# Loading x ahead of the DMA transposes, tile 3 by PE, padded K rows and a second store queue in an attention plus GLU kernel

## The chip, the cores and the metric

The kernel runs on one core of one Trainium2 chip. The metric is the device time of one execution in microseconds (us). "Span" is the time from the first to the last instruction in a profile of such an execution; it is mostly 1.7 to 2.1 us shorter than the device time of the same execution. Every execution also carries a mean granted TensorE clock, where 1.000 is full speed. Engines: PE is TensorE (matmul), DVE is VectorE, ACT is ScalarE, POOL is GpSimd, SP is SyncE, which only issues DMAs here.

## The reference

Layer norm of x, sliding dilated attention (32 heads of 20, a window of 8 keys at distance 2), and a gated bilinear unit on the un-normalized layout, summed with x. S = 2048, D = 640, F = 1536, all bf16.

```python
xn = layernorm(x)                       # x: (1, 2048, 640)
q, k, v = split(xn @ wqkv)              # 32 heads of 20
logits = q . k[s - 2*w], w = 0..7       # masked where s - 2*w < 0
A = (softmax(logits * 20**-0.5) . v[s - 2*w]) @ wo
B = ((xn @ w_gate) * (xn @ w_up)) @ w_down
return x + A + B
```

## The kernel before

The sequence is cut into 16 tiles of 128 rows. For each tile DVE takes mean and variance of a row (`ln_stats_a/b`, `ln_aggr`), normalizes (`ln_apply`), and the result XNS must be transposed into XNT, because PE needs the model dimension on partitions. Tiles 0, 1 and 2 are transposed by PE (through PSUM, copied out by ACT and DVE), tiles 3 to 15 by a DMA transpose that SP issues. The x loads, the weight loads and the transposes stand in one program order on SP's queue; some x loads are issued by ACT. PE projects Q and K of tiles 0 to 5 tile by tile, of tiles 6 and 7 with matmuls 256 wide, and of tiles 8 to 15 with matmuls 512 wide, which need four tiles at once.

```python
    x_load(1, "act"); x_load(0)
    # ... wqkv for Q, x 2 and 3, wqkv for K ...
    for t in range(4, 8):
        x_load(t)

    def ln_apply(t, between=None):
        # ... XNS[t % 4] = (x - mean) * rstd, on DVE ...
        if t >= NTP:                                    # NTP = 3
            o = XNT[:, :, t * TS:(t + 1) * TS]
            op("sp", lambda e: e.dma_start_transpose(o, xs), r=[xs], w=[o], dma=True, name=f"xT{t}")
        for u in {3: (8, 9), 4: (10,), 5: (11, 12), 6: (13,), 7: (14,), 8: (15,)}.get(t, ()):
            x_load(u, "act" if u > 11 else "sp")        # tiles 12 to 15 from ACT

    # order of the projections: (which, tile in the pair); which 0 is Q, 1 is K
    order = ((0, 0), (0, 1), (1, 0), (1, 1)) if t0 < 2 else ((0, 0), (1, 0), (0, 1), (1, 1))
    # ... tail(): the last row tile is stored in three pieces, all from SP
```

XNS has four buffers, so the normalization of tile t + 4 waits until the transpose of tile t has read its buffer. A small scheduling layer records all operations and turns overlaps of 64-byte pieces of memory into semaphore waits.

Of the kernel before, what the change touches and what calls it, by code (L numbers as in the profile page):

```python
# [18 lines left out]
PAD = (W - 1) * DIL  # L19
NT = 16  # L20
NJ = 4
TS = 128
JB = 512
DHALF = D // 2
# [4 lines left out]
HS = S // 2  # L29
SB = 256  # L30
NSB = HS // SB
KL = PAD + HS

ENGINES = ("sp", "act", "pe", "dve", "pool")
ROW_BYTES = {}
# [177 lines left out]
def build_kernel(nc, A_x, A_wqkv, A_wo, B_x, B_w_gate, B_w_up, B_w_down, out):  # L213
# [32 lines left out]
    for h in range(2):  # L246
# [3 lines left out]
        QH.append(sb(f"QH{h}", [128, NCH, HS]))  # L250
        KH.append(sb(f"KH{h}", [128, NCH, KL]))
    a_ht = place[0]
# [12 lines left out]
    NXS = 14  # L265
    XST = sb("XST", [128, NXS, D], at=a_log)
    NXN = 4
    NTP = 3
    XNS = sb("XNS", [128, NXN, D], at=a_log + NXS * D * 2)
    NXR = 2  # L270
    TLAST = 12
# [17 lines left out]
    xhbm = A_x[0]  # L289
    ohbm = out[0]  # L290

    def dma(o, i, r=(), w=(), name="", eng="sp", group=None):
        return op(eng, lambda e: e.dma_start(o, i), r=r, w=w, dma=True, name=name, group=group)
# [7 lines left out]
       r=[IDENT[:]], w=[IDENT[:]], name="ident")  # L301
# [7 lines left out]
    def x_load(t, eng="sp"):  # L309
        dma(XST[:, t % NXS, :], xhbm[t * TS:(t + 1) * TS, :], w=[XST[:, t % NXS, :]], name=f"xld{t}", eng=eng)  # L310

    wqkv_src = A_wqkv.rearrange("(c p) n -> p c n", p=128)

    def wqkv_load(g, c=None, eng="sp"):
# [12 lines left out]
        wqkv_load(1, c)  # L327
    for t in range(4, 8):
        x_load(t)

    later = []

# [24 lines left out]
    def ln_stats_a(t):  # L357
        if t >= NT:
            return
        x, st = XST[:, t % NXS, :], STATS[:, t % 2, 0:12]  # L360
        op("dve", lambda e: e.bn_stats(st[:, 0:6], x[:, 0:DHALF]), r=[x], w=[st], name=f"bna{t}")  # L361

    def ln_stats_b(t):
        if t >= NT:
            return
        x, st = XST[:, t % NXS, :], STATS[:, t % 2, 0:12]
        op("dve", lambda e: e.bn_stats(st[:, 6:12], x[:, DHALF:D]), r=[x], w=[("stb", t)], name=f"bnb{t}")  # L367

    def ln_aggr(t):
        if t >= NT:  # L370
            return
        st, mv, sd = STATS[:, t % 2, 0:12], MV[:, t, 0:2], SD[:, t, 0:1]
        op("dve", lambda e: e.bn_aggr(mv, st), r=[st, ("stb", t)], w=[mv], name=f"bnag{t}")  # L373
        op("act", lambda e: e.activation(sd, mv[:, 1:2], ACT.Sqrt, bias=EPSC[:, 0:1]), r=[mv, EPSC[:]], w=[("sd", t)],  # L374
           name=f"sd{t}")
# [13 lines left out]
    def ln_rstd(t):  # L389
        if t >= NT:  # L390
            return
        sd, rstd = SD[:, t, 0:1], SD[:, t, 1:2]
        op("dve", lambda e: e.reciprocal(rstd, sd), r=[("sd", t)], w=[("rstd", t)], name=f"rstd{t}")  # L393

    def ln_apply(t, between=None):
        if t >= NT:
            return
        x, xs, mv = XST[:, t % NXS, :], XNS[:, t % NXN, :], MV[:, t, 0:2]
        sd, rstd = SD[:, t, 0:1], SD[:, t, 1:2]
        op0 = ALU.add if t == 1 else ALU.subtract  # L400
        mean = ("nm", t) if t == 1 else mv
        if between is None:
            ln_rstd(t)
        else:
            between()
        for c0, c1 in ((0, 128), (128, D)) if t == 0 else ((0, D),):
            o, i = xs[:, c0:c1], x[:, c0:c1]
            op("dve", (lambda o, i: lambda e: e.tensor_scalar(o, i, mv[:, 0:1], rstd, op0=op0, op1=ALU.mult))(o, i),  # L408
               r=[i, mean, ("rstd", t)], w=[o], name=f"lnap{t}")
        if t >= NTP:  # L410
            o = XNT[:, :, t * TS:(t + 1) * TS]
            op("sp", lambda e: e.dma_start_transpose(o, xs), r=[xs], w=[o], dma=True, name=f"xT{t}")
        for u in {3: (8, 9), 4: (10,), 5: (11, 12), 6: (13,), 7: (14,), 8: (15,)}.get(t, ()):
            x_load(u, "act" if u > 11 else "sp")
        if t == NT - 1:
            late_loads()

# [230 lines left out]
    stores = []  # L648
    fin_bank = [0]

    def tail(t, nb):
        j, rows = t // 4, slice((t % 4) * TS, (t % 4 + 1) * TS)
        flush_h(0)
        n = NF + NCH
        last = t == NT - 1
        parts = ((0, DHALF - 64), (DHALF - 64, 64)) if last and nb == 1 else ((0, DHALF),)
        for h, wid in parts:
            b = bank()
            c0 = nb * DHALF + h
            cols = slice(c0, c0 + wid)  # L660
            for i in range(n):
                if i < NF:
                    l, x = ht(j, i)[:, rows], WD[:, i, cols]
                else:
                    l, x = VO[:, i - NF, t * TS:(t + 1) * TS], WO[:, i - NF, cols]
                op("pe", (lambda l, x, i, b, wid: lambda e: e.matmul(PS[:, b, 0:wid], l, x, start=(i == 0), stop=(i == n - 1)))(l, x, i, b, wid),  # L666
                   r=[l, x], w=[PS[:, b, :]], name=f"dn{t}_{nb}_{i}")
            if t < TLAST:
                if nb == 0:
                    fin_bank[0] = b  # L670
                    continue
                assert b == fin_bank[0] + 1
                o = FACC[:, t % NFO, :].rearrange("p (n d) -> p n d", n=2)
                i = PS[:, b - 1:b + 1, 0:wid]
                op("act", (lambda o, i: lambda e: e.activation(o, i, ACT.Copy))(o, i),  # L675
                   r=[PS[:, b - 1, :], PS[:, b, :]], w=[o], name=f"fin{t}")
                continue
            o = FOUT[:, t % NFO, cols]
            xr = XR[:, t % NXR, cols]
            op("dve", (lambda o, xr, b, wid: lambda e: e.tensor_tensor(o, PS[:, b, 0:wid], xr, ALU.add))(o, xr, b, wid),  # L680
               r=[PS[:, b, :], xr], w=[o], name=f"fin{t}_{nb}")
            if last:
                stores.append(dma(ohbm[t * TS:(t + 1) * TS, cols], o, r=[o], name=f"odma{t}_{c0}"))
        if nb == 1 and t < TLAST:
            if t % 2 == 0:
                return
            f = FACC[:, (t - 1) % NFO:(t - 1) % NFO + 2, :]
            d = ohbm[(t - 1) * TS:(t + 1) * TS, :].rearrange("(u p) n -> p u n", p=TS)
            stores.append(op("pool", lambda e: e.dma_start(d, f, accum_op=ALU.add), r=[f, ("out",)], w=[("out", t)],  # L689
                             dma=True, name=f"oacc{t}"))  # L690
        elif nb == 1 and not last:
            f = FOUT[:, t % NFO, :]
            stores.append(dma(ohbm[t * TS:(t + 1) * TS, :], f, r=[f], name=f"odma{t}"))
            if t + NXR < NT:
                xr_load(t + NXR)
# [20 lines left out]

    def tr(t):
        ln_pe(t)
        if t == 1:
            ln_copy(t)  # L720
        if t < 3:
            ln_stats_a(t + 1)
            ln_stats_b(t + 1)
            ln_aggr(t + 1)
        if t > 1:
            ln_copy(t)
        if t < 3:
            ln_apply(t + 1)

    n_ln = [4]  # L730
    t_ln = [12.3]

    def ln_pace(t):
        while t_ln[0] <= t and n_ln[0] < NT:
            u = n_ln[0]
            if u == 4:
                ln_stats_a(4)
                ln_stats_b(4)
                ln_aggr(4)
            ln_stats_a(u + 1)  # L740
            ln_stats_b(u + 1)
            ln_rstd(u)
            ln_apply(u, lambda: ln_aggr(u + 1))
            n_ln[0] += 1
            t_ln[0] += 1.45

    tp = 6.8
    for t0 in (0, 2, 4):
        bm = bank() if t0 == 4 else None
        if t0 == 2:  # L750
            bank_ring[:] = [5, 0, 6, 7, 2, 1, 3, 4]
            bm = bank()
        order = ((0, 0), (0, 1), (1, 0), (1, 1)) if t0 < 2 else ((0, 0), (1, 0), (0, 1), (1, 1))
        at = {(0, 0): (3, lambda: tr(1)), (1, 0): (3, lambda: tr(2))}
        for which, dt in order:
            t = t0 + dt
            b = bank()
            if t0 == 0:
                if bm is None:
                    bm = bank()  # L760
                proj_tile(which, t, b, bm, (2 * which + t) * TS, at.get((which, t)))
            else:
                proj_part(which, t, (0, 1), b, 0)
                proj_part(which, t, (2, 3), b, 2 * TS)
                proj_part(which, t, (4,), bm, (2 * which + dt) * TS)
            part_evac(which, t, 1, 0, 4, b, 0)
            tp += 1.4
            if (which, dt) == (1, 1):
                for u in (0, 1):
                    part_evac(u, t0, 2, 4, 1, bm, 2 * u * TS)  # L770
            ln_pace(tp)
# [19 lines left out]
    def exp_preload():  # L791
        op("act", lambda e: e.activation(DUM[:, 0:1], EPSC[:, 0:1], ACT.Exp), r=[EPSC[:]], w=[DUM[:]], name="exp_preload")

    t_pe, t_dve = [31.0], [33.2]
    fill, pos = [], [0]
    pv_done = [0]
    loaded = []
# [164 lines left out]
```

## Time and profile before

| | before |
|---|---|
| device time, median of the first 3 runs | 256.66 us (256.22 to 256.66) |
| span of the profiled run | 254.3 us, clock 1.000 |
| PE busy | 98% |
| first real matmul of the projections / last matmul | 6.1 us / 251.9 us |

The page of the profile, busy time of the engines and the chain of work that ended last by engine (shares of the span):

```profile
PE 249.0 (98%) x1618; PEld 148.8 (59%) x1618; DVE 215.4 (85%) x251; ACT 114.2 (45%) x203; POOL 35.9 (14%) x44
...
PE 92%; DMA 5%; DVE 1%; ACT 1%; issue 0%; SPq 0%
```

PE is the limit. The 5% of DMA in the chain is, in order of time, the first x load (2.72 us), the load of tile 10 (4.28) and the transpose of tile 7 behind it (5.50); the last two are what the change aims at. The view of waits of PE shows where PE stands still for a transpose (us in total, times, longest):

```profile
PE PS L478 <- DMA XNT<-XNS: 1.6, 1, 1.6
PE PS L441 <- DVE EPSC L297: 1.0, 1, 1.0
```

L478 is the tile-by-tile projection, `XNT<-XNS` a DMA transpose. The timeline of PE shows where it is (start us, us, engine, line, operation, what, count, idle time before):

```profile
12.29 8.54 PE L478 MATMUL PS<-XNT,WQKV 128*128 128x128 bf16 x150
22.48 2.96 PE L478 MATMUL PS<-XNT,WQKV 128*128 128x128 bf16 x50 [1.65 <-DMA XNT<-XNS]
25.57 5.66 PE L496 MATMUL PS<-XNT,WQKV 128*128 128x256 bf16 x50
31.06 1.24 PE L463 MATMUL PS<-XNT,WQKV 128*128 128x512 bf16 x5
```

The matmuls of tile 5 start at 22.48 although the ones before were through at 20.83. The transposes of tiles 4 to 7, issued between 14.4 and 20.1 us, and how long they took from issue to landing:

```profile
L412 SPq DMA_TRANSPOSE XNT<-XNS x4: 1205/1250/1742, 14.5 to 20.0; - x4
...
DMA to landing us min/median/max: 2.9/5.7/6.9
```

One by one, from the semaphore increments in the trace (a DMA counts its semaphore up in 16 steps; at the sixteenth it has landed): tile 4 took 2.91 us, tile 5 5.98, tile 6 6.90, tile 7 5.50. The DMA queues between 17 and 19 us (q1 is SP's queue, q10 ACT's, q8 fetches instructions; packets, MB, share of the 16 engines' time in this stretch, over 100% where packets overlap):

```profile
q1 hardware_dynamic: 513, 0.26, 90.7%
q10 hardware_dynamic: 148, 0.17, 61.5%
q8 instruction: 1, 0.02, 2.8%
```

The end of the kernel: the last two stores are issued one behind the other by SP, the second one at 252.30 (in the trace), 0.1 us after its data.

```profile
251.92 0.81 SPq L293 DMA_DIRECT2D out_dram<-FOUT  x2
251.97 0.23 DVE L680 TENSOR_TENSOR FOUT<-PS,XR 128x64 bf16<-128x64 f32 x1
```

### The profile page before, as it was taken

Reading aid. Unit: us, or ns where it says so; the run is one execution under the profiler, and the core shown is the slowest. Engines: PE = TensorE matmul, PEld = TensorE weight load, DVE = VectorE, ACT = ScalarE, POOL = GpSimd, SP = SyncE. Lnnn points to the kernel's source line nnn. Section 1 sums busy time; section 2 is a strip of 40 time slices with the busy share of each in tenths; the row PEclk is TensorE's granted clock in tenths of the full one; section 3 lists DMA queues with packets and bytes.
Section 4 is the critical chain, followed back from the end, with each engine's and each line's share of the span. In section 5 each row is a group of like instructions: output and inputs, shape, how many; then the busy total and the mean of one; then the engine's idle time right before and its main releaser. Section 6 shows DMA issues by size and latency. Waiting matters only on the chain.

```text
span 254.3 us, 3924 instructions
## 1 busy us (share of the span) xinstructions
PE 249.0 (98%) x1618; PEld 148.8 (59%) x1618; DVE 215.4 (85%) x251; ACT 114.2 (45%) x203; POOL 35.9 (14%) x44
## 2 busy tenths in 40 slices
PE   8997999999999999999999999999999999999996
PEld 3996955555554444444444447764444777777775
DVE  4795999999999962999999995799999999996221
ACT  6574666555555557555555552325555112112000
POOL 1000001024344422002222101101000010111000
PEclk9999999999999999999999999999999999999999
DMA  6799869947784673264458961294000021430511
GB/s 204 262 179 186 106 125 400 313 126 134 144 146 80 128 124 62 76 256 83 82 106 253 403 227 24 18 359 59 0 0 0 3 19 33 54 39 15 103 52 53
DMA packets 26369, 32.01 MB, mean 126 GB/s; under 512 B 10576, under 2 KB 22864, under 8 KB 26320
## 3 DMA queue, kind: packets, MB, share of 16 engines
q1 hardware_dynamic: 19392, 21.64, 28.0%
q0 software_dynamic: 6240, 9.31, 23.4%
q10 hardware_dynamic: 720, 0.82, 1.6%
q8 instruction: 12, 0.20, 0.3%
q14 instruction: 5, 0.04, 0.0%
HBM read 14.42 MB, written 4.59 MB: 75 GB/s over the span
## 4 chain that ended last, share of the span: by engine, by line
PE 92%; DMA 5%; DVE 1%; ACT 1%; issue 0%; SPq 0%
PE PS L635 41%; PE PS L666 29%; PE PS L463 17%; DMA XST<-in_A_x_dram 3%; PE PS L489 2%; PE PS L496 2%; DMA XNT<-XNS 2%; DVE XNS L408 0%; PE PS L422 0%; ACT KH L504 0%; ACT XNS L381 0%; DVE SD L393 0%; DVE STATS L361 0%; DVE STATS L367 0%; ACT SD L374 0%; DVE MV L373 0%
## 5 line engine op out<-in xcount | busy, mean ns | idle before, releaser
L635 PE MATMUL PS<-XNT,WU 128*128 128x512 bf16 x240 | 59.6, 379 | 0.0
L635 PE MATMUL PS<-XNT,WG 128*128 128x512 bf16 x240 | 59.6, 379 | 0.0
L602 DVE TENSOR_TENSOR PVB<-VO,ATB 128x10240 f16<-128x10240 bf16 x8 | 43.9, 5489 | 0.2
L463 PE MATMUL PS<-XNT,WQKV 128*128 128x512 bf16 x200 | 43.3, 379 | 0.0
L666 PE MATMUL PS<-WD,HT 128*128 128x320 bf16 (+2 forms) x300 | 43.2, 294 | 0.0
L635 PEld LDWEIGHTS PS<-XNT,WU 128*128 128x128 bf16 x240 | 23.5, 98 | 28.3
L635 PEld LDWEIGHTS PS<-XNT,WG 128*128 128x128 bf16 x240 | 23.5, 98 | 28.2
L637 ACT ACTIVATE USX<-PS 128x512 bf16<-128x512 f32 x48 | 28.7, 597 | 22.6 <-PE PS L635 22.1
L666 PEld LDWEIGHTS PS<-WD,HT 128*128 128x128 bf16 x300 | 28.7, 98 | 11.0
L463 PEld LDWEIGHTS PS<-XNT,WQKV 128*128 128x128 bf16 x200 | 23.5, 118 | 19.5
L597 DVE TENSOR_TENSOR PVB<-PVB 128x5120 f16<-128x5120 f16 (+1 forms) x16 | 34.5, 2156 | 0.3
L530 POOL DMA_DIRECT2D LOG<-PE x24 | 21.6, 928 | 60.3 <-DMA LOG<-PE 60.1
L637 ACT ACTIVATE HT<-PS 128x512 bf16<-128x512 f32 x36 | 21.5, 597 | 16.3 <-PE PS L635 16.3
L675 ACT ACTIVATE FACC<-PS 128x640 f16<-128x640 f32 x12 | 8.5, 704 | 44.3 <-PE PS L666 44.3
L666 PE MATMUL PS<-WO,VO 128*128 128x320 bf16 (+2 forms) x165 | 27.1, 295 | 0.0
L666 PEld LDWEIGHTS PS<-WO,VO 128*128 128x128 bf16 x165 | 15.9, 98 | 5.9
L519 DVE TENSOR_TENSOR TMP<-QH,KH 128x2048 f16<-128x2048 bf16 x16 | 19.1, 1219 | 0.0
L519 DVE TENSOR_TENSOR PP<-QH,KH 128x2048 f16<-128x2048 bf16 x16 | 18.9, 1219 | 0.0
L524 DVE TENSOR_TENSOR PP<-PP,TMP 128x4096 f16<-128x4096 f16 x8 | 18.3, 2291 | 0.2
L530 POOL DMA_DIRECT2D PE<-PP x8 | 8.7, 1090 | 63.6 <-DVE PP L525 63.6
L689 POOL DMA_DIRECT2D out_dram<-FACC x6 | 7.1, 1186 | 74.7 <-ACT FACC L675 74.7
L680 DVE TENSOR_TENSOR FOUT<-PS,XR 128x320 bf16<-128x320 f32 (+2 forms) x9 | 4.1, 455 | 15.3 <-PE PS L666 15.2
(67 smaller groups left out, 227.0 us busy)
## 6 DMA issues: line engine op xcount, KB each, us to landing
PE<-PP POOLq DMA_DIRECT2D x8, 512.0 KB, 5.0
ATB<-LOG SPq DMA_DIRECT2D x8, 512.0 KB, 4.3
LOG<-PE POOLq DMA_DIRECT2D x24, 128.0 KB, 2.7
WG<-in_B_w_gate_dram SPq DMA_DIRECT2D x5, 384.0 KB, 6.3
WU<-in_B_w_up_dram SPq DMA_DIRECT2D x5, 384.0 KB, 11.1
WD<-in_B_w_down_dram SPq DMA_DIRECT2D x1, 1920.0 KB, 10.3
out_dram<-in_A_x_dram SPq DMA_DIRECT2D x1, 1920.0 KB, 9.2
out_dram<-FACC POOLq DMA_DIRECT2D x6, 320.0 KB, 4.9
```

The costliest lines, as they stand in the source:

```text
L463: op("pe", (lambda l, x, c: lambda e: e.matmul(PS[:, b, :], l, x, start=(c == 0), stop=(c == NCH - 1)))(l, x, c), r=[l, x], w=[PS[:, b, :] ...
L489: op("pe", (lambda o, l, x, st, sp: lambda e: e.matmul(o, l, x, start=st, stop=sp))(o, l, x, st, sp), r=[l, x], w=[o], name=f"pp{which}_{m ...
L519: return (1.22, lambda: op("dve", lambda e: e.tensor_tensor(o, qw, kw, ALU.mult), r=[q, k], w=[o], name=f"prod{h}_{p}_{c}"))
L524: (2.3, lambda: op("dve", lambda e: e.tensor_tensor(a, a, b, ALU.add), r=[a, b], w=[a], name=f"psum{h}_{p}")),
L530: op("pool", lambda e: e.dma_start(o, i, accum_op=ALU.add), r=[o, i], w=[o], dma=True, name=name)
L597: return lambda: op("dve", lambda e: e.tensor_tensor(o, x, y, ALU.add), r=[x, y], w=[o], name=f"{name}_{b}")
L602: lambda: op("dve", lambda e: e.tensor_tensor(PVB[:], vw, aw, ALU.mult), r=[v, a], w=[PVB[:]], name=f"pv_{b}")),
L635: op("pe", (lambda l, x, c: lambda e: e.matmul(PS[:, b, :], l, x, start=(c == 0), stop=(c == NCH - 1)))(l, x, c), r=[l, x], w=[PS[:, b, :] ...
L637: op("act", lambda e: e.activation(o, PS[:, b, :], ACT.Copy), r=[PS[:, b, :]], w=[o], name=f"guev{which}_{m}_{j}")
L666: op("pe", (lambda l, x, i, b, wid: lambda e: e.matmul(PS[:, b, 0:wid], l, x, start=(i == 0), stop=(i == n - 1)))(l, x, i, b, wid), r=[l, ...
L675: op("act", (lambda o, i: lambda e: e.activation(o, i, ACT.Copy))(o, i), r=[PS[:, b - 1, :], PS[:, b, :]], w=[o], name=f"fin{t}")
L689: stores.append(op("pool", lambda e: e.dma_start(d, f, accum_op=ALU.add), r=[f, ("out",)], w=[("out", t)], dma=True, name=f"oacc{t}"))
```

## The change

The intent is to have x in SBUF before the transposes start, so that no load stands between transposes 4 to 7, with tiles 8 to 11 and 14, 15 loaded in pairs. Tile 3 is transposed by PE, so that SP's queue has no transpose in it until tile 4. All x loads but that of tile 1 are now issued by SP: ACT no longer issues loads 12 to 15. KH rows are padded to a multiple of 64 bytes. The next to last store piece goes out from ACT. Constants of the static scheduler are adjusted.

```diff
-KL = PAD + HS
+KL = (PAD + HS + 31) // 32 * 32
-    NTP = 3
+    NTP = 4
+    def x_load2(t):
+        dst = XST[:, t % NXS:t % NXS + 2, :]
+        dma(dst, xhbm[t * TS:(t + 2) * TS, :].rearrange("(u p) n -> p u n", p=TS), w=[dst], name=f"xld{t}")
     for t in range(4, 8):
         x_load(t)
+    x_load2(8)
+    x_load2(10)
+    x_load(12)
@@ ln_apply
-        for u in {3: (8, 9), 4: (10,), 5: (11, 12), 6: (13,), 7: (14,), 8: (15,)}.get(t, ()):
-            x_load(u, "act" if u > 11 else "sp")
+        if t == 7:
+            x_load(13)
+            x_load2(14)
@@ tail
-                stores.append(dma(ohbm[...], o, r=[o], name=f"odma{t}_{c0}"))
+                eng = "act" if c0 == DHALF else "sp"
+                stores.append(dma(ohbm[...], o, r=[o], name=f"odma{t}_{c0}", eng=eng))
@@ order of the projections; tile 3 is transposed inside the last one of tiles 0 and 1
-        order = ((0, 0), (0, 1), (1, 0), (1, 1)) if t0 < 2 else ((0, 0), (1, 0), (0, 1), (1, 1))
-        at = {(0, 0): (3, lambda: tr(1)), (1, 0): (3, lambda: tr(2))}
+        order = ((0, 0), (0, 1), (1, 0), (1, 1)) if t0 < 4 else ((0, 0), (1, 0), (0, 1), (1, 1))
+        at = {(0, 0): (3, lambda: tr(1)), (1, 0): (3, lambda: tr(2)), (1, 1): (4, lambda: tr(3))}
-    t_pe, t_dve = [31.0], [33.2]
+    t_pe, t_dve = [30.3], [31.2]
# cut: tr() and ln_pace() in the form that fits tile 3 on PE, t_ln 12.3 -> 12.6
```

More of the change, by code (lines that the diff above doesn't have):

```diff
@@ L682, in tail @@
             if last:
-                stores.append(dma(ohbm[t * TS:(t + 1) * TS, cols], o, r=[o], name=f"odma{t}_{c0}"))
+                eng = "act" if c0 == DHALF else "sp"
+                stores.append(dma(ohbm[t * TS:(t + 1) * TS, cols], o, r=[o], name=f"odma{t}_{c0}", eng=eng))
         if nb == 1 and t < TLAST:
@@ L718, in tr @@
         ln_pe(t)
-        if t == 1:
+        if t != 2:
             ln_copy(t)
-        if t < 3:
-            ln_stats_a(t + 1)
-            ln_stats_b(t + 1)
-            ln_aggr(t + 1)
-        if t > 1:
+        ln_stats_a(t + 1)
+        ln_stats_b(t + 1)
+        ln_aggr(t + 1)
+        if t == 2:
             ln_copy(t)
@@ L730, in build_kernel @@
     n_ln = [4]
-    t_ln = [12.3]
+    t_ln = [12.6]
     def ln_pace(t):
@@ L735, in ln_pace @@
             u = n_ln[0]
-            if u == 4:
-                ln_stats_a(4)
-                ln_stats_b(4)
-                ln_aggr(4)
             ln_stats_a(u + 1)
```

## The prediction

> **What bounds the kernel now.** TensorE does: the page shows PE busy 98% of a 254.3 us span, and the chain that ended last is 92% PE. The view of PE's waits has two entries: 1.0 us at the start (before any data exists) and one stall of 1.6 us, "PS L478 <- DMA XNT<-XNS". The timeline puts it at 20.83 to 22.48 us: the projection of tile 5 waits for its DMA transpose. From 25.57 us (after a second wait of some 0.13 us for tiles 6 and 7) to 251.9 us PE never stops. So only the head (0 to 31 us) and the last store can pay.
>
> **Cause of the stall.** Read issue by issue, the DMA records show that transposes issued while no x load is in flight, or before it, land 2.7 to 2.9 us after issue (tile 3, tile 4). Those of tiles 5, 6 and 7, issued at 16.4, 18.2 and 20.0 us between the x loads of tiles 10 to 15, take 6.0, 6.9 and 5.5 us, and the loads take 4.5 to 5.4 instead of 2.7 to 4.0. VectorE, not PE alone, then waits: 1.0 us twice before the normalization of tiles 9 and 10, for their buffers, which those late transposes are still reading. The Trainium skill (DMA: Bandwidth & Descriptors, Rules for kernel authors) says a transpose next to ordinary DMAs "needs nothing"; that is about correct data, and this trace shows that it costs time.
>
> **What the change does, with costs.**
> - Loads of tiles 8 to 12 go out before any transpose. x loads stream at about 0.45 us a tile (landings of tiles 4 to 7: 10.86 to 12.17), so they should be in by about 14.5 us. Transposes 4 to 7 then run without loads: about 2.8 us each. Tile 4 issued near 14.0 lands near 17 (wanted 18.3); tile 5 near 18.3 (wanted 21.1); tile 7 near 21 (wanted 24.0). The 1.65 + 0.13 us stall goes.
> - Tile 3 by PE: five more 128x128 transposes, 0.28 us of PE (as for tiles 1 and 2 in the chain), plus one 0.69 us eviction on ACT, which has slack.
> - Loads 13 and 14+15 are still before transposes 8 to 11; those are wanted at about 29.4 us instead of 31.06. I expect tile 11 in by 27 to 29: little margin, the main risk.
> - VectorE's normalizations end about 2 us earlier, so the logits start near 30.4 instead of 32.13. PE's program after the head is unchanged.
> - KH padding: the products take 1.22 us before, and rows 64-byte aligned should not change that; it removes false dependencies only. About 0.
> - Last store: the 16 KB store was issued at 252.30, 0.1 us after its data, behind the other store's issue. Two queues: 0.1 to 0.15 us. The skill (same page, "Issuing engines are not separate DMA queues") says two issuers save only issue time, which is this size.
>
> **Sum on the critical path.** -1.78 + 0.28 - 0.12 = -1.6 us of 256.66: 255.1 us, with 254.3 to 256.1 in 8 of 10. Faster by over 2%: 1%; within 2%: 98%; slower: 1%.
>
> **What would show it.** No PE wait for XNT in the head; transposes of tiles 4 to 7 under 3.5 us; the 256-wide projections start at 24.0 (before 25.57) and the 512-wide ones at 29.4 (before 31.06); the span falls by the same amount; last store issued by 252.2 minus that shift.
>
> **What would make it wrong.** Transposes 8 to 11 slowed by loads 13 to 15, so PE stalls before the 512-wide projections (gain 0.8 us or less); transposes slow of themselves, not through mixing; a new wait in mid-kernel from the shifted VectorE order.

## The result and the profile after

The kernel after takes 254.49 us (median of 6 runs, 254.27 to 254.76), against 256.66 us (6 runs, 256.22 to 257.52). Ratio 0.9911, 95% interval 0.9895 to 0.9927: 0.9% less, inside the range. Ratios here are the mean time of one kernel's fast runs over that of the other's of the same rounds, so not quite the ratio of the medians.

The page after (the lines that answer to those of before):

```profile
PE 249.1 (99%) x1623; PEld 149.3 (59%) x1623; DVE 214.7 (85%) x251; ACT 114.8 (45%) x204; POOL 35.9 (14%) x44
...
PE 99%; DVE 0%; issue 0%
```

The chain is PE alone now, with 5 more matmuls (the transposes of tile 3). Of PE's waits only the one at the start is left:

```profile
PE PS L449 <- DVE EPSC L297: 1.0, 1, 1.0
```

The timeline of PE over the same stretch:

```profile
12.68 11.33 PE L486 MATMUL PS<-XNT,WQKV 128*128 128x128 bf16 x200
23.85 5.62 PE L504 MATMUL PS<-XNT,WQKV 128*128 128x256 bf16 x50
29.31 2.97 PE L471 MATMUL PS<-XNT,WQKV 128*128 128x512 bf16 x13
```

The 200 narrow matmuls run without a break, the 512-wide ones start 1.75 us earlier (31.06 to 29.31), and nothing waits after that: the last matmul of the chain ends at 250.19 instead of 251.95. Transposes 4 to 7:

```profile
L419 SPq DMA_TRANSPOSE XNT<-XNS x4: 1198/1266/1452, 14.2 to 18.6; - x4
...
DMA to landing us min/median/max: 2.9/3.3/4.3
```

One by one: 2.95, 4.33, 3.56 and 2.86 us. The queues between 17 and 19 us have no q10 any more, but the instruction fetch is still there:

```profile
q1 hardware_dynamic: 1065, 0.27, 100.2%
q8 instruction: 1, 0.02, 3.3%
```

The end:

```profile
250.17 0.35 ACTq L293 DMA_DIRECT2D out_dram<-FOUT  x1
250.46 0.33 SPq L293 DMA_DIRECT2D out_dram<-FOUT  x1
```

So the span fell by 1.8 us (254.3 to 252.5), about what was predicted (1.6), while the median times fell by 2.2. Two questions are left: what exactly made the transposes slow, since tile 5's still takes 4.33 us although the last load landed at 16.58, 0.7 us after its issue; and where the other 0.4 us come from. (The profiled execution of before took 256.07 us, 0.6 us less than the median from which the prediction subtracts; that of after, 254.55, lies at its median.)

### The profile page after: what moved, and what is told of

Same layout as the page of the kernel before. It is cut to its first block, busy times and chain, and to the rows that moved or that the text cites. A ratio compares the mean times of both kernels' runs of the same rounds, so it can differ in the third digit from the quotient of the medians.

```text
span 252.5 us, 3929 instructions
## 1 busy us (share of the span) xinstructions
PE 249.1 (99%) x1623; PEld 149.3 (59%) x1623; DVE 214.7 (85%) x251; ACT 114.8 (45%) x204; POOL 35.9 (14%) x44
## 4 chain that ended last, share of the span: by engine, by line
PE 99%; DVE 0%; issue 0%
PE PS L643 41%; PE PS L674 29%; PE PS L471 17%; PE PS L486 4%; PE PS L497 2%; PE PS L504 2%; PE PS L449 2%; PE PS L430 1%; DVE FOUT L688 0%; DVE ZERO L296 0%; DVE EPSC L297 0%
```

## The experiments

Theories at the outset. A: any x load among the transposes slows them; the change takes the loads out. F (B in the first runs): DMA fetches of instructions slow them, loads do not matter. C: moving tile 3 to PE is what helped. D: the padding or the store queue carries a part. A further one, R, came later. "Wanted" in the expectations is the time at which PE would come to the tile if nothing had stalled it. "One run" means a single profiled execution: its latencies and stalls can be read, its time carries no interval.

**Loads alone.** Kernel before with the new loads, tile 3 still by DMA.

```diff
+    x_load2(8)
+    x_load2(10)
+    x_load(12)
-        for u in {3: (8, 9), 4: (10,), 5: (11, 12), 6: (13,), 7: (14,), 8: (15,)}.get(t, ()):
-            x_load(u, "act" if u > 11 else "sp")
+        if t == 7:
+            x_load(13)
+            x_load2(14)
```

> Kernel before with the x loads of the change alone (8 to 12 ahead, 13 and 14+15 behind transpose 7); tile 3 is still transposed by DMA. Theory A (x loads among the transposes cost the stall; the PE transpose of tile 3 is only what makes room for it): transposes 5 to 7 take 3 to 4.4 us instead of 5.5 to 6.9, the stall before tile 5 goes, but tile 3's transpose now stands behind loads that land until 16.6 us in the kernel after, so it lands at 16 to 17 us instead of 14.4 and PE, which wants it at 15.14, stalls 1 to 2 us there: time within 0.4 us of before. Rival B (the loads do not matter, the DMA instruction fetches do): tile 3's transpose takes 2.7 us as before and there is no stall at tile 3, or the stall before tile 5 stays.

Measured: 255.41 us (4 runs: 255.40, 255.41, 255.41 and 258.04), ratio 0.9978, interval 0.9909 to 1.0047. In the profile tile 3's transpose took 5.91 us behind the loads, which landed until 16.87, and PE waited 1.9 us for it; transposes 4 to 6 took 3.2, 2.6 and 2.6 us, and 7, with a fetch at 19.91 in its flight, 4.0. As expected: the loads ahead of the transposes free tiles 5 to 7 and bury tile 3 (the median time, 0.7 us under before, fell more than the 0.4 that was expected at most). The PE transpose of tile 3 is what makes room.

This profile (the 258.04 us run) shows a second effect. Its granted clock is 0.993, and by stretches (columns: us, busy PE, PEld, DVE, ACT, POOL, then granted clock, DMA share, GB/s):

```profile
15.00:18.40 3.40, 1.48 (x27) 1.33 (x25) 3.40 (x14) 1.29 (x4) 0.00 (x0) 1.00 0.61 116
18.40:21.80 3.40, 3.40 (x36) 3.40 (x34) 1.24 (x4) 0.61 (x2) 0.00 (x0) 0.50 0.95 92
21.80:25.00 3.20, 3.20 (x60) 3.20 (x59) 1.85 (x8) 2.43 (x7) 0.00 (x0) 1.00 0.61 166
```

From 0.9 us after the stall PE ran 3.4 us at half clock: 36 matmuls in 3.4 us, against 60 in the 3.2 us after it. Half of 3.4 us is a loss of 1.7 us, on top of the stall.

**Tile 3 by PE alone.** Kernel after with the loads put back among the transposes (12 to 15 from ACT), no padding, one store queue.

```diff
-    x_load2(8)
-    x_load2(10)
-    x_load(12)
-        if t == 7:
-            x_load(13)
-            x_load2(14)
+        for u in {3: (8, 9), 4: (10,), 5: (11, 12), 6: (13,), 7: (14,), 8: (15,)}.get(t, ()):
+            x_load(u, "act" if u > 11 else "sp")
-KL = (PAD + HS + 31) // 32 * 32
+KL = PAD + HS
-                eng = "act" if c0 == DHALF else "sp"
+                eng = "sp"
-    t_pe, t_dve = [30.3], [31.2]
+    t_pe, t_dve = [31.0], [33.2]
```

> Kernel before with tile 3 transposed by PE alone: x loads 8 to 15 stand among the transposes as before, no KH padding, one store queue. Theory A: transposes 5 to 7 still take 5 us or more, PE stalls 1 to 1.5 us before tile 5 or 6, and 0.28 us of PE transposes come on top: time 0 to 0.4 us above before. Rival C (taking tile 3 out of the DMA transposes is what freed the queue): the stall goes and the time falls by 1.2 us or more.

Measured: 255.77 us (255.04 to 256.60), ratio 0.9978, interval 0.9915 to 1.0041; span of the profiled run 253.2. Neither side was right. Transposes 5, 6 and 7 are still slow (5.42, 4.91, 4.02 us), but the stall before tile 5 shrank; the chain (start us, us, what) shows 0.8 us of it (0.5 by the view of waits, which showed 1.65 before):

```profile
12.85 8.11 PE PS L482 x145
20.96 0.02 issue
20.98 0.60 ACT KH L508
21.58 0.19 ACT SD L378
21.77 2.94 PE PS L482 x50
```

The profile puts this wait down to ACT; tile 5's transpose landed at 21.62 in the trace, so I take it to be the transpose. With tile 3 off SP's queue, loads 8 and 9 were issued at 8.8 instead of 13.1 us. My expectation of no gain or a loss was a miss in the profile; in the times the interval leaves it open.

**One batch behind tile 3.** Kernel after, tile 3 by DMA as before, loads 8 to 15 as four pairs right behind it.

```diff
-    NTP = 4
+    NTP = 3
-    x_load2(8)
-    x_load2(10)
-    x_load(12)
-        if t == 7:
-            x_load(13)
-            x_load2(14)
+        if t == 3:
+            for u in (8, 10, 12, 14):
+                x_load2(u)
# and tr(), order and at of the kernel before
```

> Kernel after, but tile 3 by DMA transpose as before (no PE transposes of it), and all x loads 8 to 15 as four pairs in one batch right behind that transpose and ahead of transpose 4. Theory A: tile 3 lands by 14.5 as in before, the batch lands between about 15 and 18.5, transposes 4 and 5 suffer a little from it (4 to 5 us), tile 4 lands at 18.5 to 19 against 18.0 wanted: stall 0.5 to 1 us, later ones none; time 255.3 to 255.9, no better than after. If the loads cost nothing to transposes of their own queue that stand behind them: no stall, 0.28 us under after (span near 252.2).

Measured: 260.18 us (259.82 to 260.77), ratio 1.0141, interval 1.0087 to 1.0195: slower by 1.4%, much more than expected. The batch landed only at 21.54, with an instruction fetch at 19.49 in it; transpose 4 behind it took 6.85 us; PE stalled 4.2 us, and the clock fell (0.987 to 0.993 in all four runs). Here the transpose behind the loads on its own queue landed only after all of them. Why the last two pairs took 1.8 and 2.4 us each, where the second took 0.9, I did not settle.

**All loads ahead.** Kernel after, loads 13 to 15 also ahead of transpose 4.

```diff
-        if t == 7:
+        if t == 3:
             x_load(13)
             x_load2(14)
```

> Kernel after with loads 13 and 14+15 also ahead of transpose 4. Theory A: with no load in flight, transposes 8 to 11 take 2.7 to 2.9 us except one that an instruction fetch (16 KB packet) falls into (4 us or more); in the kernel after they took 3.2 to 4.6. PE does not wait for them in either: span within 0.1 us of 252.5. If the loads land later than 17 us, transpose 4 is late (over 3.5 us) and PE may stall at tile 4 (wanted 18.3). Rival B: the latencies of transposes 8 to 11 do not change.

Measured: one run, 254.78 us, span 252.7, no stall. The transposes issued from 20 to 26 us (8 to 11) took 2.6, 2.8, 3.8 and 3.3 us (kernel after: 3.8, 4.6, 3.8, 3.2). The slow one, tile 10's, is the one with a fetch (24.72 us) in its flight. Both the loads and the fetch are visible; PE waits for neither. Tile 5's transpose, issued at 16.14 with loads landing until 17.04, still took 4.40 us, with a fetch at 18.14.

**Moving the fetches.** In both kernels the warm-up gets more PE instructions for the same time, so that PE's 16 KB instruction fetches come at other moments.

```diff
-    warm(10)
+    warm_waits(30, 2)      # 30 matmuls 128 wide, each behind two waits that are already satisfied
+    warm(2)
```

> Kernel before with more PE instructions in the warm-up (30 narrow matmuls with 2 satisfied waits each and 2 wide ones for 10 wide ones): the same work follows, but PE's instruction fetches (16 KB packets, at 10.95, 17.99, 26.74 us before) come 1 to 5 us earlier. The x loads stand as before. Theory F (the fetch at 18 us freezes the transpose of tile 5; loads among transposes add little): with the fetch out of 16.4 to 20.5 us, tile 5's transpose lands 3 to 4.4 us after issue, no stall before tile 5, time 1.0 us or more under before. Theory A (loads among transposes): it still takes 5 us or more and PE stalls 1 us or more before tile 5 or 6. Both in part: 4.4 to 5 us, stall 0.2 to 0.8. If PE starts its real work later than 5.6 us, the wanted times shift by that.

> Kernel after with the same longer warm-up. No x load is in flight from 16.6 to 20 us. Theory F: the transpose that took 4.33 us (tile 5, fetch at 17.92) takes 2.6 to 3.2 us now, and the 1 to 1.5 us go to whichever transpose the moved fetch falls into (probably tile 4 or tile 7). If transposes slow down for another reason: tile 5 still takes over 4 us. Span 252.3 to 253.2: a fetch in tile 4's transpose can make PE wait some tenths at tile 4 (wanted 18.3).

Measured for the kernel after: one run, 254.15 us, span 252.4. The fetch moved from 17.92 to 15.09 us; PE's first projection started at 6.0, as before. The transposes of tiles 4 to 7:

```profile
L419 SPq DMA_TRANSPOSE XNT<-XNS x4: 1276/1299/1467, 14.2 to 18.6; - x4
...
DMA to landing us min/median/max: 2.6/2.8/3.6
```

Tile 5's took 2.86 us instead of 4.33, tile 4's, into which the fetch now fell, 3.60 instead of 2.95. No load moved in the program, but the loads of tiles 8 to 12 landed by 15.27 instead of 16.58, since the fetch before this one moved too. The run without padding and second store queue (below) excludes that this is what helped: there the loads were in by 15.29, no load was in flight, the fetch came at 18.12, and tile 5's transpose took 4.10 us. So the fetch is a cause.

The trace hints at how. In the kernel after, an ordinary load under a fetch (tiles 8 and 9, fetch at 12.79) had 15 of its 16 semaphore increments by 13.57 us and the last at 15.24. Tile 5's transpose under the fetch at 17.92 had all 16 increments between 20.11 and 20.23, and 19 of its 256-byte packets on SP's queue, starting at 18.85 to 19.12, took 0.7 to 1.0 us each, where such packets mostly take 0.02. My reading is that a fetch keeps one DMA engine busy, and that it then holds up one part of a load but the whole of a transpose, as if the 16 engines proceeded in lockstep; no run tests this by itself.

Measured for the kernel before: the fetch moved from 17.99 to 15.99 us. In the profiled run (255.01 us, span 253.2) tile 5's transpose took 4.31 us instead of 5.98 and did not stall PE; tile 4's took 4.28 instead of 2.91 and now stalled PE for 0.9 us. So the fetch's share moved from tile 5 to tile 4, and the rest of tile 5's delay stayed (4.31 against 2.6 to 2.9 undisturbed): both theories hold in part. How much of this rest is due to loads this run does not say: tile 5's transpose also stood in line behind tile 4's (landed 18.90) and load 10 (19.82), which the fetch had made late. The times of this kernel were no better (257.03, ratio 1.0007, interval 0.9949 to 1.0064): its three other runs had spans of 254.9 to 256.0 at full clock. They were not profiled, so why they differ from the profiled one is open.

**Padding and store queue undone.** Kernel after without these two.

```diff
-KL = (PAD + HS + 31) // 32 * 32
+KL = PAD + HS
-                eng = "act" if c0 == DHALF else "sp"
+                eng = "sp"
```

> Kernel after without the KH padding and without the second store queue. Main theory: both are worth next to nothing: ratio to before 0.990 to 0.993 as after had (0.9911); in the profile the last store is issued 0.1 us after its data instead of 0.03, span 252.6 to 252.7; the first product starts 0.3 to 0.7 us later than the 29.79 of after, off the critical path. Rival D (the padding or the store queue carried the surplus over the 1.6 us that were predicted): ratio 0.993 to 0.995.

Measured: 254.58 us (254.51 to 254.89), ratio 0.9922, interval 0.9879 to 0.9966; span 252.8. Nearly the whole gain is there without them. The interval alone would also allow D's 0.993 to 0.995, but the four spans of 252.7 to 252.8, against 252.5 to 252.7 of the kernel after, leave the two together at most 0.3 us, so D falls. In the profile the last store is issued at 250.77 and lands at 252.32, 0.12 us later relative to the start of the 512-wide projections than in the kernel after (252.32 - 29.54 against 251.97 - 29.31). The first product started at 30.39 instead of 29.79; 0.2 us of that is a later head. PE waits for neither.

**Three loads behind transpose 4, from SP and from ACT.** Kernel after, loads 13 to 15 behind transpose 4, from either queue.

```diff
# from SP                              # from ACT
-        if t == 7:                    -        if t == 7:
+        if t == 4:                    -            x_load(13)
             x_load(13)                -            x_load2(14)
             x_load2(14)               +        if t == 4:
                                       +            for u in (13, 14, 15):
                                       +                x_load(u, "act")
```

> Kernel after with the loads of tiles 13, 14 and 15 issued behind transpose 4 instead of behind transpose 7: nothing else differs. Theory A: transposes 5 to 7 go from 4.3, 3.6 and 2.9 us back to 5 us or more, tile 5 lands at 21.5 to 23 against 21.1 wanted, PE stalls 0.4 to 1.8 us. Theory F (fetches alone): latencies stay within 0.6 us of after's and there is no stall.

Measured from SP: one run, 255.61 us, but a span of 252.6 and no stall for XNT. Tiles 5, 6 and 7 took 4.28, 3.70 and 2.75 us, against 4.33, 3.56 and 2.86: no change. A fetch (17.68) fell into tile 5's flight here as well. Theory A falls in this form: what the loads on the same queue cost the transpose behind them is its place in line (tile 5 was issued 0.85 us later and landed at 21.03 instead of 20.23).

The kernel before issues loads 12 to 15 from ACT, and this made theory R: a load on the second queue is not held in line, it runs beside a transpose that is already under way, and the two slow each other. The Trainium skill (DMA: Bandwidth & Descriptors, Queues, rings and completion order) says that each DMA engine goes round-robin between the queue rows that have work, a packet at a time. The stretch from 17 to 19 us before agrees in that both queues moved packets in it (513 of q1 and 148 of q10); that they take turns packet by packet the trace does not show.

> Kernel after with loads 13, 14 and 15 behind transpose 4 as in the run before it, but issued from ACT as three single loads. Theory R: they share the DMA engines with transposes 5 and 6: transpose 5 takes 5 us or more (4.28 with the same loads on SP), 6 and 7 over 4 us, tile 5 lands at 21 to 22 us (wanted 21.1) and PE may stall up to 0.9 us. If the ring does not matter: transpose 5, issued about 15.9, takes 4.3 to 4.9 us.

Measured from ACT: one run, 256.02 us, span 254.1. ACT does not wait behind transpose 4, so the loads went out at 14.1 to 14.9 us and it was tile 4's transpose that they met. Tile 4's transpose, first with the loads from SP, then from ACT:

```profile
L419 SPq DMA_TRANSPOSE XNT<-XNS x1: 1322/1322/1322, 14.3 to 14.3; - x1
...
DMA to landing us min/median/max: 2.7/2.7/2.7
```

```profile
L419 SPq DMA_TRANSPOSE XNT<-XNS x1: 1322/1322/1322, 14.3 to 14.3; - x1
...
  PE PS L486: 1.1, 1
...
DMA to landing us min/median/max: 5.2/5.2/5.2
```

The next fetch came at 19.70, after tile 4 had landed (19.50), so these 2.5 us are the loads. PE stalled 1.1 us, and the span is 1.6 us longer than that of the kernel after: nearly the whole gain is gone. Tile 5 took 5.86 and tile 6 5.06 us. The loads differ from those of the run before not only in their queue: they also went out some 1.6 us earlier, beside the transpose instead of behind it. A load ahead does not do it by itself: in the kernel before, loads 8 and 9 stood ahead of tile 4's transpose on its own queue and landed until 16.41, and it took 2.91 us.

**One load queue, in the kernel before.** Its single edit:

```diff
-            x_load(u, "act" if u > 11 else "sp")
+            x_load(u)
```

> Kernel before, its one edit: the loads of tiles 12 to 15 are issued from SP, at the same places among the transposes, instead of from ACT. Theory R (what loads cost is the second ring: loads on ACT's queue are served in turn with a transpose that is already under way, while loads on the transposes' own queue only take their place in line): tile 5's transpose, which then has tile 10's load alone ahead of it, lands at 20.3 to 21.2 us instead of 22.34 although the fetch at 18 us still falls into it; PE stalls 0 to 0.4 us before it instead of 1.65; tile 6 and 7 land by 24.5 (wanted 24 to 25.4). Time 0.8 to 1.6 us under before (ratio 0.994 to 0.997). Theory A (any load among the transposes does it): tile 5 lands at 22 or later, no gain.

Measured: 256.44 us (256.19 to 256.58), ratio 0.9977, interval 0.9929 to 1.0024; span 254.6. Half of it came true. Tile 5's transpose took 4.27 us instead of 5.98, landed at 20.61 although a fetch (17.69) fell into it, and did not stall PE. But the time is no better, because the stall moved (waits of PE):

```profile
PE PS L463 <- DMA XNT<-XNS: 1.5, 1, 1.5
...
PE PS L496 <- DMA XNT<-XNS: 0.6, 1, 0.6
```

SP now issues four more loads between its transposes, some 0.6 us each, and everything behind them is later: tile 11's transpose is issued at 28.60 instead of 27.07, and the 512-wide projections wait 1.5 us for it. I had looked only at tiles 5 to 7. This is what loading in pairs and ahead is for.

**A candidate.** Kernel after, tile 3 by DMA again (saves the 0.28 us of PE), all loads as pairs from SP, spread out; and the kernel after again beside it.

```diff
-    NTP = 4
+    NTP = 3
-    x_load2(10)
-    x_load(12)
-        if t == 7:
-            x_load(13)
-            x_load2(14)
+        if t in (3, 5, 7):
+            x_load2({3: 10, 5: 12, 7: 14}[t])
# and tr(), order and at of the kernel before
```

> A candidate from the findings: kernel after, but tile 3 by DMA transpose again (saves 0.28 us of PE), all loads on SP in pairs (8+9 ahead of transpose 3, 10+11 behind it, 12+13 behind transpose 5, 14+15 behind transpose 7), none from ACT. Theory R with the fetch: transposes take 2.7 us alone, 3 to 4.3 with a fetch or a pair of loads ahead; tile 3 lands at 14.5 to 15.5 (wanted 15.1), tile 5 by 20.8, tile 11 by 29: stalls of 0 to 0.5 us in all. Ratio to before 0.989 to 0.993, within 0.2% of the kernel after in the same call; a clear gain over after is not expected. If a load pair costs a transpose of its own queue more than its line time, tile 4 or 5 comes 1 us late and the ratio is over 0.994.

> The kernel after unchanged, beside the candidate and the kernel before on one chip: ratio to before 0.990 to 0.993 again; its runs within 0.5 us of each other, all at clock 1.0, while one or two of before's show a granted clock of 0.993 and a span some 2 us longer.

Measured: the candidate 254.89 us (254.06 to 256.20), ratio 0.9934, interval 0.9899 to 0.9969; the kernel after 254.37 (254.23 to 254.86), ratio 0.9915, interval 0.9885 to 0.9945. The candidate's best run has a span of 252.3, its profiled one 254.4, with tile 4's transpose at 5.31 us (pair 10+11 ahead of it, a fetch at 18.32 in it) and a stall of 1.8 us. Its best span (252.3) is 0.1 us under the best of the kernel after (252.4), its worst (254.4) 2.0 us over it; that the good runs are those in which nothing collides is likely, but they were not profiled. It does not beat the kernel after, whose runs stay within 0.6 us of each other.

This also settles the surplus as far as it can be. Of the 11 runs of before, two show a clock of 0.993 and spans of 256.2; the other nine have 0.999 or more and spans of 253.5 to 255.3. The mean of those nine is 256.24, of all eleven 256.55; the mean of the six of after is 254.46. So the gain is 1.78 us at full clock, the same as between the two profiled spans, and 2.09 with the clock drops counted. Over all, 7 of 32 runs of before were at 0.993, and none of the 12 runs of after.

## Why the prediction was right, point by point

- **Time.** Predicted 255.1 (254.3 to 256.1), measured 254.49. "Within 2%" was right. The gain was 2.2 us by the medians where 1.6 was forecast; by the two profiled executions (256.07 and 254.55) it was 1.5, by their spans 1.8.
- **The stall goes, the program after the head is unchanged.** Right: no PE wait for XNT; 256-wide projections at 23.85 (forecast 24.0), 512-wide at 29.31 (29.4).
- **"-1.78" for the stall: the term that was too small.** I took PE's idle time after the modelled end of the last matmul. By pace it was more: 200 narrow matmuls run from 12.68 to 23.85 in the kernel after, 11.17 us, and from 12.29 to 25.57 before, 13.28 us. The stalls cost 2.11 us. With the PE transposes and the start (12.68 - 12.29 = 0.39 us, of which 0.28 is the five transposes) that gives 1.72 us at the 256-wide projections, and the span fell by 1.8.
- **The clock.** Not in the prediction at all. One stall of 1.9 us was followed by 3.4 us at half clock (granted clock 0.993). 2 of the 11 runs of before show 0.993 as well, worth 0.3 us of the mean there; they were not profiled, so that a stall did it there too is inferred. It does not explain the first comparison: the clock of those runs is not on record, but every run of before at 0.993 in the later calls took 257.77 us or more, and the six of the first took at most 257.52. Those six are 0.15 to 1.45 us above the profiled execution, and full-clock runs of before differ by as much later (spans 253.5 to 255.3). Why they do is open, and with it most of the 0.4 us.
- **Cause of the slow transposes: right in direction, wrong in kind.** "Transposes issued while no x load is in flight, or before it, land 2.7 to 2.9 us after issue" is not what held: tile 5's, with loads in flight for its first 0.7 us only, still took 4.33 us (4.10 with none in flight, in the run without padding and second store queue), and two of the four missed my mark of 3.5. The trace of before spoke against the reading already: tile 4's transpose, which the prediction counts as undisturbed, had loads 8 and 9 ahead of it on its queue until 16.41. Two causes add up to the 5.98 us of before: an instruction fetch during the flight (4.33 to 2.86 when moved away) and loads on the second queue beside it (5.98 to 4.27 when sent from SP, and 2.7 to 5.2 for tile 4 when put on ACT in the kernel after). Loads on the transposes' own queue, which I blamed too, cost their place in line (4.28 against 4.33). The change takes both kinds of load away from transposes 4 to 7 at once, so the forecast came true without depending on which kind does the harm: that much of it was luck.
- **"They should be in by about 14.5 us."** They landed at 15.24, 16.11 and 16.58, mostly because of the fetch at 12.79: 15 of the 16 increments of the last one were in by 14.86. Harmless: DVE did not wait for them.
- **Tile 11 "in by 27 to 29".** 28.33, 1.0 us ahead of need.
- **Tile 3 by PE.** 0.28 us as forecast. The runs add what it buys: without it, loads ahead bury tile 3 (a stall of 1.9 us).
- **KH padding, about 0.** Right for the time as far as is known (it was undone only together with the second store queue, at most 0.3 us for both); the products take 1.22 us in both kernels.
- **Last store, 0.1 to 0.15.** 0.12 between the profiles with one queue and two. It agrees with the skill's statement, cited in the prediction, that a second issuer saves only issue time.

## What to carry to other kernels

While a DMA transpose that PE waits for is in flight, keep plain loads off the other DMA queue. Put them on the transpose's own queue, in few large issues, and so early that they land before the transpose is wanted: a whole batch right ahead of one cost a stall of 4.2 us here. Leave slack of 1.5 us (4.33 against 2.86) for an instruction fetch that you do not control: the candidate, whose schedule was tighter, had the better best run and the worse median (254.89 against 254.37). When you size a stall, compare the pace of the same instructions with and without it, and look at the granted clock of every run: in one profiled run a stall of 1.9 us was followed by a loss of 1.7 at half clock. And when a change removes two suspects at once, put each back alone before you name the cause.

## What the Trainium skill lacked or had wrong

- DMA: Bandwidth & Descriptors, Rules for kernel authors: "A transpose next to ordinary DMAs needs nothing." For correct data, yes; for time it lacks that plain loads on the other hardware queue took a transpose from 2.7 to 5.2 us, while loads of the same tiles behind it on its own queue left it at 2.7.
- Runtime: NRT & Kernel Launch, Instruction fetch mechanics, says that crossing a 16 KiB block costs little and is mostly hidden. PE itself did not wait for its fetches here, but a DMA transpose in flight did: 4.33 us with the fetch, 2.86 with it moved away. A plain load with a fetch in its flight had one of its 16 increments late (15.24 against 13.57 us).
- TensorE: Matmul & The Clock Gate, Why this matters for your kernels, asks for no PE idle gaps over about 3 us. Here a gap of 1.9 us was followed by 3.4 us at half clock in one profiled run; gaps of 1.65 and 1.8 us in two others were not. PE had been busy for 1.49 us of the 3.41 us before the drop, and for 1.63 us of those that end at 20.40 in the run with the 1.8 us gap; two runs give no threshold. The page's 3.4 us window (Part 1) agrees with the 3.4 us at clock 0.50.
